# Moving token sums, a turned tile and the last store in a float32 attention and gated-MLP kernel on one Trainium2 core

## The chip, the cores and the metric

The kernel runs on one core of a Trainium2 chip. A core has TensorE (PE, matrix products into the banks of PSUM), VectorE (DVE), ScalarE (ACT), GpSimd (POOL) and SyncE (SP); SP, ACT and POOL also issue the DMA transfers. The engines run at the same time, each works through its own instructions in order, and semaphores make one wait for another. The metric is the device time of one execution in microseconds (us). Before the change it is 1393.94 us, the median of three runs.

## The reference

Two layers, each an attention block A and a gated MLP block B, on 2048 tokens of 512 features, all in float32. `layernorm` takes mean and variance over the last axis.

```python
def A(x, wqkv, wo):                       # 32 heads of 16
    q, k, v = split(x @ wqkv)
    pq, pk = phi(q), phi(k)               # phi(t) = (t + 1 if t > 0 else exp(t)) + 1e-6
    kv = einsum("bhsd,bhse->bhde", pk, v)
    z = einsum("bhsd->bhd", pk)
    num = einsum("bhqd,bhde->bhqe", pq, kv)
    den = einsum("bhqd,bhd->bhq", pq, z)[..., None] + 1e-6
    return merge(num / den) @ wo

def B(x, w_in, w_sp, b_sp, w_out):        # w_in 512 x 1792, w_sp 2048 x 2048
    z = gelu(x @ w_in)
    z1, z2 = z[..., :896], layernorm(z[..., 896:])
    g = w_sp @ z2 + b_sp[:, None]
    return (z1 * g) @ w_out

x = x + A(layernorm(x)); x = x + B(layernorm(x))
x = x + A(layernorm(x)); x = x + B(layernorm(x))
```

## The kernel before

**Numbers.** A float32 operand is split into a high part (ACT, `high`, L101) and the rest (DVE or POOL, `low`, L104); `mm3` (L115 to L117) makes one product out of three matmuls on these parts. So each operand costs PE a wait for ACT first, and for DVE at the third matmul.

**Memory.** `Slots` hands out tiles by hand: 22 pages (`pg`, 128 x 512 floats), 6 quads (`qd`), 4 bigs (`bg`) and 8 PSUM banks. A freed tile goes to the end of its list; who gets it next waits for its last users. The order of every engine's work is the order of the calls in the Python code.

**Stages.** The 2048 tokens are 16 blocks of 128. Each layer has these stages:

- `P1`: blocks are loaded, normalised and turned (`T`, in a high and a low half), then multiplied by the weights for K and Q. `start` (first layer) loads the first blocks and eight weight pieces, fills the wait of PE with `idle` matmuls on constants (L434), and interleaves the splits of the pieces (`wk.piece`) with the first blocks. Blocks 0 to 2 of the first layer are turned on PE (L247), all others by a store, a load and a transpose on DVE (L286).
- `P2`: steps `s` = 1 to 18. A step takes block `s` through `b`, block `s - 1` through `c` (a product, an addition L643, statistics, `c3` with a store and the turning) and block `s - 2` through `d` (turned and split into `xT`, one quad each for the high and low parts of four blocks). Block `s - 3` goes through `e` (24 matmuls with 448 columns, two gelus L700, statistics L222), block `s - 4` through `e4` (normalised). Products `f` with the other half of `w_in` are made for four blocks at a time.
- `P4`: 56 steps of products with `w_sp`, then `o(i)` for 16 blocks: product, addition L1198, store L1200. `join` starts the next layer's `P1` in the last steps of the first layer: `T(0)` in step 14 and `T(1)` in step 15.

**The seven products.** In the second layer (`self.seven`) the `f` products of the last eight blocks are made as seven products of half-size parts (P1 to P7). Four of these need sums of tokens of two blocks: block 8 + k, kept in `xT[2]`, and block 12 + k, just turned (`y`). In `d_low` of blocks 12 to 15, steps 14 to 17, `block_sums` (L755 to L758) writes the four sums; the full value of block 8 + k comes from `whole`, which adds its high and low part on POOL (L743) a step ahead. `block_parts(m, p)` splits the sums into the quads `Tp[m]`, in two halves `p`. `side(s)` sets what of this a step does: products P1 and P2 (`P1(g)`, `P2(g)`, six matmuls each, L791 to L793), with copies (L799), the addition L813 and gelus (L733); the splits; and `fetch_sum`, three DMAs on POOL's queue (L773), which bring weight sums stored in DRAM by the first layer. `tail` then makes P3 to P7, and each product waits for its `Tp` and its fetched sums.

**Sums of `w_sp`.** In the first layer `sums.tick()` (steps 8 to 18 and some of `P4`) loads pieces of `w_sp`, adds them on POOL (L978) and stores the sums.

Of the kernel before, what the change touches and what calls it, by code (L numbers as in the profile page):

```python
# [10 lines left out]
F32 = mybir.dt.float32  # L11
# [42 lines left out]
def mixer_kernel(ctx: ExitStack, tc: tile.TileContext, x_in, wqkv, wo_d, win1_d, win2_d, wsp_d, bsp_d, wout_d,  # L54
# [236 lines left out]
    class P1:  # L291
# [124 lines left out]
        def start(self):  # L416
# [19 lines left out]
            idle(10)  # L436
# [3 lines left out]
            self.wk.piece()  # L440
            self.T_high(0)
            idle(4)
# [3 lines left out]
            self.wk.piece()  # L446
# [122 lines left out]
    class P2:  # L569
        def __init__(self, p1):  # L570
# [8 lines left out]
            self.S, self.T, self.Tp = {}, {}, {}  # L579
# [92 lines left out]
        def d_low(self, i):  # L672
# [3 lines left out]
            if self.seven and n == 3:  # L676
                self.block_sums(k, b)
            home.put(b)
# [34 lines left out]
        def f(self):  # L713
# [8 lines left out]
            if f == NF - 1 and not (self.seven and n == 3):  # L722
                quads.put(*self.xT.pop(n))
# [15 lines left out]
        def whole(self, k):  # L739

            h, l = (t[:, :, k * P:(k + 1) * P].bitcast(F32) for t in self.xT[2])
            self.xr = pages.get([P, 4, P])
            nc.gpsimd.tensor_tensor(self.xr, h, l, op=OP.add)  # L743

        def block_sums(self, k, y):


            p, o = divmod(k, 2)
# [4 lines left out]
            x = self.xr  # L753
# [5 lines left out]
            pages.put(x)  # L759
# [42 lines left out]
        def P1(self, g):  # L802
            if g == 0:
                self.X, self.C = [], []
            self.X.append(banks.get(PAGE))
            self.product(self.X[g], "P1", g, start=True)
            self.C.append(self.copied(self.X[g]))

        def P2(self, g):
            y = banks.get(PAGE)  # L810
            self.product(y, "P2", g, start=True, stop=True)
            t = self.C[g]
# [48 lines left out]
        def side(self, s):  # L861

            if s == 14:
                self.P1(0)
                self.P1(1)
            elif s == 15:
                self.P1(2)
                self.P2(0)
                self.fetch_sum(4)
            elif s == 16:  # L870
                self.P2(1)
                self.P2(2)
# [12 lines left out]
            if 13 <= s < 17:  # L885
                self.whole(s - 13)

        def run(self, sums):
            w1 = self.win1
            for s in range(1, NT + 3):  # L890
# [16 lines left out]
                else:  # L907
# [37 lines left out]
                w1.fetch()  # L945
                if s > 7:
# [54 lines left out]
    class P4:  # L1001
# [189 lines left out]
        def o(self, i):  # L1191
# [6 lines left out]
            nc.vector.tensor_add(x, x, b)  # L1198
# [119 lines left out]
```

## Time and profile before

| | before |
|---|---|
| device time, three runs | 1392.9, 1393.94, 1395.38 us; median 1393.94 us |
| the profiled execution | 1392.76 us, its span 1391.0 us |
| PE (matmuls) busy | 1383.0 us, 99% of the span, 6252 matmuls |
| DVE busy | 908.8 us, 65% |
| ACT busy | 595.1 us, 43% |
| POOL busy | 429.2 us, 31% |
| chain of work that ended last | PE 96%, DVE 2%, ACT 1%, POOL 1%, issue 1% |
| DMA | 233.57 MB, mean 168 GB/s |

The span is the time from the first to the last instruction of the profile; the device time of the same execution is 1.76 us longer. In the rows below, a row of the timeline gives the start and the duration in us, the engine (PEld is the load of a matmul's weights, `SPq` an issue of a DMA by SP), the line of the kernel, what is written and read, a count, and in brackets for how long the engine was idle before and what ended that. Neighbouring instructions of one kind can be merged into one row with their count. PE's busy time is modelled: matmuls overlap, so two starts may lie closer together than one matmul lasts.

### The profile page before, as it was taken

The page shows a single profiled execution, that of the slowest core. Times are in us where ns is not written, and L with a number is a line of the kernel's source. Part 1 is how long each engine was busy: PE and PEld are TensorE (multiplying, and loading weights), DVE is VectorE, ACT ScalarE, POOL GpSimd, SP SyncE. Part 2 cuts the span into 40 slices and gives each one's busy share as a digit, 9 for nine tenths or more (in the row PEclk, how much of TensorE's full clock was granted, in tenths as well). Part 3 has the DMA queues.
Part 4 walks back from the last instruction along what each step waited for, and adds up shares of the span by engine and source line. Part 5 has one row for each costly group of instructions (what it writes and reads, how often), then busy time and mean ns, then how long its engine had stood idle before and what let it go on. Part 6 is the DMA issues. An engine that isn't in the chain of part 4 may idle for free.

```text
span 1391.0 us, 17707 instructions
## 1 busy us (share of the span) xinstructions
PE 1383.0 (99%) x6252; PEld 1159.9 (83%) x6252; DVE 908.8 (65%) x1305; ACT 595.1 (43%) x922; POOL 429.2 (31%) x518
## 2 busy tenths in 40 slices
PE   9999999999999999999999999999999999999998
PEld 7888888888888888888888888888878888888887
DVE  6785777853755587666667767876666345776642
ACT  6674543444442234241366755444454432342410
POOL 3343344544135541431023424432320001123310
PEclk9999999999999999999999999999999999999999
DMA  5541256766678864357745313555454323434442
GB/s 174 171 132 59 91 167 224 260 228 211 212 246 287 297 228 137 122 203 241 266 130 177 112 45 122 174 175 173 124 187 152 106 91 129 174 129 159 167 145 90
DMA packets 148313, 233.57 MB, mean 168 GB/s; under 512 B 12416, under 2 KB 54144, under 8 KB 148224
## 3 DMA queue, kind: packets, MB, share of 16 engines
q1 hardware_dynamic: 144768, 226.15, 49.0%
q0 software_dynamic: 1728, 3.15, 0.8%
q10 hardware_dynamic: 1728, 3.15, 0.6%
q8 instruction: 49, 0.80, 0.2%
q14 instruction: 40, 0.33, 0.1%
HBM read 161.35 MB, written 71.04 MB: 167 GB/s over the span
## 4 chain that ended last, share of the span: by engine, by line
PE 96%; DVE 2%; ACT 1%; POOL 1%; issue 1%; ACTq 0%; POOLq 0%
PE bank L117 18%; PE bank L116 18%; PE bank L115 18%; PE bank L1105 13%; PE bank L1104 13%; PE bank L1103 13%; PE bank L247 1%; PE bank L793 0%; PE bank L792 0%; PE bank L791 0%; DVE st L222 0%; PE bank L434 0%; ACT qd L101 0%; ACT pg L235 0%; DVE pg L286 0%
## 5 line engine op out<-in xcount | busy, mean ns | idle before, releaser
L1104 PE MATMUL bank<-qd,pg 128*128 128x512 f32 x800 | 311.2, 389 | 0.0
L1105 PE MATMUL bank<-qd,pg 128*128 128x512 f32 x800 | 311.2, 389 | 0.0
L1103 PE MATMUL bank<-qd,pg 128*128 128x512 f32 x800 | 311.2, 389 | 0.0
L1069 DVE TENSOR_TENSOR qd<-qd,qd 128x1024 fp32r<-128x1024 f32 x112 | 158.4, 1414 | 138.7 <-ACT qd L1062 138.5
L1062 ACT ACTIVATE qd<-qd 128x1024 fp32r<-128x1024 f32 x112 | 118.6, 1059 | 235.9 <-DMA qd<-s 96.5
L1125 POOL TENSOR_TENSOR bg<-bg,pg 128x512 f32<-128x512 f32 x56 | 78.2, 1399 | 327.6 <-DMA pg<-z 302.9
L1104 PEld LDWEIGHTS bank<-qd,pg 128*128 128x128 f32 x800 | 150.2, 188 | 31.4
L1103 PEld LDWEIGHTS bank<-qd,pg 128*128 128x128 f32 x800 | 150.2, 188 | 31.3
L1105 PEld LDWEIGHTS bank<-qd,pg 128*128 128x128 f32 x800 | 150.2, 188 | 30.8
L117 PE MATMUL bank<-qd,pg 128*128 128x512 f32 x384 | 149.9, 390 | 0.0
L226 POOL TENSOR_SCALAR rs<-mv 128x1 f32<-128x1 f32 x96 | 38.5, 401 | 333.5 <-DVE mv L224 320.3
L978 POOL TENSOR_TENSOR pg<-pg,pg 128x512 f32<-128x512 f32 x64 | 93.7, 1464 | 93.8 <-DMA pg<-in_wsp_dram 85.4
L235 ACT ACTIVATE pg<-pg,nb,rs 128x512 f32<-128x512 f32 x63 | 51.1, 811 | 161.8 <-POOL nb L229 155.6
L115 PE MATMUL bank<-qd,pg 128*128 128x512 f32 x288 | 112.3, 390 | 0.0
L116 PE MATMUL bank<-qd,pg 128*128 128x512 f32 x288 | 112.2, 390 | 0.0
L115 PE MATMUL bank<-bg,qd 128*128 128x448 f32 x256 | 94.2, 368 | 1.6 <-ACT qd L101 1.6
L117 PE MATMUL bank<-bg,qd 128*128 128x448 f32 x256 | 93.6, 366 | 0.1
L116 PE MATMUL bank<-bg,qd 128*128 128x448 f32 x256 | 93.6, 366 | 0.0
L101 ACT ACTIVATE pg<-pg 128x512 fp32r<-128x512 f32 (+1 forms) x83 | 51.0, 616 | 96.5 <-DVE pg L286 51.9
L115 PE MATMUL bank<-wo,qd 128*128 128x512 f32 x224 | 87.1, 389 | 0.0
L116 PE MATMUL bank<-wo,qd 128*128 128x512 f32 x224 | 87.1, 389 | 0.0
L117 PE MATMUL bank<-wo,qd 128*128 128x512 f32 x224 | 87.1, 389 | 0.0
(156 smaller groups left out, 2689.7 us busy)
## 6 DMA issues: line engine op xcount, KB each, us to landing
qd<-s SPq DMA_DIRECT2D x64, 512.0 KB, 3.4
qd<-in_wsp_dram SPq DMA_DIRECT2D x48, 512.0 KB, 4.2
pg<-in_wsp_dram SPq DMA_DIRECT2D x64, 256.0 KB, 5.0
s<-pg SPq DMA_DIRECT2D x64, 256.0 KB, 4.8
pg<-x SPq DMA_DIRECT2D x64, 256.0 KB, 3.3
pg<-z SPq DMA_DIRECT2D x56, 256.0 KB, 3.7
x<-pg SPq DMA_DIRECT2D x48, 256.0 KB, 2.6
z<-pg SPq DMA_DIRECT2D x44, 256.0 KB, 2.9
```

Source lines behind the costliest of these rows:

```text
L101: nc.scalar.activation(h, src, AF.Copy)
L115: nc.tensor.matmul(out, ah, bh, start=start, stop=False)
L116: nc.tensor.matmul(out, ah, bl, start=False, stop=False)
L117: nc.tensor.matmul(out, al, bh, start=False, stop=stop)
L235: nc.scalar.activation(y, x, AF.Identity, bias=nb, scale=rs)
L978: nc.gpsimd.tensor_tensor(t, a, b, op=OP.add)
L1062: nc.scalar.activation(w[:, 0], r, AF.Copy)
L1069: nc.vector.tensor_sub(w[:, 1], r, w[:, 0].bitcast(F32))
L1103: m(out, h[:, o], w[:, 0, j, :], start=start, stop=False, skip_group_check=True)
L1104: m(out, h[:, o], w[:, 1, j, :], start=False, stop=False, skip_group_check=True)
L1105: m(out, l[:, o], w[:, 0, j, :], start=False, stop=stop, skip_group_check=True)
L1125: nc.gpsimd.tensor_tensor(u, u, z1, op=OP.mult)
```

## The change

- `start`: 8 and 2 idle matmuls where there were 10 and 4; the second weight piece is split before the high half of block 0's turned tile, where it came after its low half.
- Second layer, steps 13 to 18: `whole` goes away. `d_low` of blocks 12 to 15 only keeps `y` (`held`); `block_sums` takes it a step later, steps 15 to 18, after `d` and before `e4`, and adds the high and low part of block 8 + k itself, on DVE.
- `side`: P1(g) in steps 14, 15, 16 and P2(g) in steps 15, 16, 17, one each (before: two P1 in step 14, one of each in step 15, two P2 in step 16). All splits are in steps 17 (two) and 18 (six), where they were in steps 16, 17 and 18. The three fetches go to steps 16, 17, 18 (before 15, 16, 17). `xT[2]` is given back in step 18.
- First layer: one `sums.fetch()` already in step 7.
- `join`: `T(1)` of the next layer comes before `o(15)` instead of after it.
- The last output block of the second layer is added and stored in two halves of 256 columns, one store on SP's queue and one on ACT's.

```diff
-            idle(10)
+            idle(8)
             self.ln_a(0)
             self.ln_a(1)
             self.ln_b(0)
             self.wk.piece()
+            self.wk.piece()
             self.T_high(0)
-            idle(4)
+            idle(2)
             banks.put(b)
             pages.put(m, f)
             self.T_low(0)
-            self.wk.piece()
             self.ln_b(1)
...
             if self.seven and n == 3:
-                self.block_sums(k, b)
-            home.put(b)
+                self.held.append((k, b))
+            else:
+                home.put(b)
...
-        def whole(self, k):
-
+        def block_sums(self):
+
+
+            if not self.held:
+                return
+            k, y = self.held.popleft()
+            x = pages.get([P, 4, P])
             h, l = (t[:, :, k * P:(k + 1) * P].bitcast(F32) for t in self.xT[2])
-            self.xr = pages.get([P, 4, P])
-            nc.gpsimd.tensor_tensor(self.xr, h, l, op=OP.add)
-
-        def block_sums(self, k, y):
-
-
+            nc.vector.tensor_add(x, h, l)
...
-            if s == 14:
-                self.P1(0)
-                self.P1(1)
-            elif s == 15:
-                self.P1(2)
-                self.P2(0)
+            if 15 <= s < 18:
+                self.P2(s - 15)
+            if 14 <= s < 17:
+                self.P1(s - 14)
+            if s == 16:
                 self.fetch_sum(4)
-            elif s == 16:
-                self.P2(1)
-                self.P2(2)
-                self.fetch_sum(2)
-                for m in (2, 3):
-                    self.block_parts(m, 0)
             elif s == 17:
                 self.last_f(2)
-                self.block_parts(2, 1)
-                self.block_parts(3, 1)
+                self.block_parts(2, 0)
+                self.block_parts(3, 0)
+                self.fetch_sum(2)
+            elif s == 18:
+                quads.put(*self.xT.pop(2))
+                for m, p in ((2, 1), (3, 1), (4, 0), (4, 1), (1, 0), (1, 1)):
+                    self.block_parts(m, p)
                 self.fetch_sum(3)
-            elif s == 18:
-                for m in (4, 1):
-                    for p in range(2):
-                        self.block_parts(m, p)
-            if 13 <= s < 17:
-                self.whole(s - 13)
...
+                if s >= 15:
+                    self.block_sums()
                 if s >= 4:
                     self.e4(s - 4)
...
+                if s == 7:
+                    sums.fetch()
                 if s > 7:
                     sums.tick()
...
-            nc.vector.tensor_add(x, x, b)
+            out = xs[2 * self.L + 2, i]
+            if self.L == 1 and i == NT - 1:
+                for issue, s in ((nc.sync, slice(0, 256)), (nc.scalar, slice(256, 512))):
+                    nc.vector.tensor_add(x[:, s], x[:, s], b[:, s])
+                    issue.dma_start(out[:, s], x[:, s])
+            else:
+                nc.vector.tensor_add(x, x, b)
+                nc.sync.dma_start(out, x)
             banks.put(b)
-            nc.sync.dma_start(xs[2 * self.L + 2, i], x)
...
+                if i == NT - 1 and nxt is not None:
+                    nxt.T(1)
                 self.o(i)
...
-            if i == 15:
-                nxt.T(1)
```

More of the change, by code (lines that the diff above doesn't have):

```diff
@@ L578, in __init__ @@
             self.seven = self.L == 1
-            self.S, self.T, self.Tp = {}, {}, {}
+            self.held = deque()
+            self.S, self.T, self.Tp, self.X = {}, {}, {}, {}
         def loadx(self, i):
@@ L721, in f @@
                 mm3(b, (w.h[:, f, c, :], w.l[:, f, c, :]), (h[:, c, :], l[:, c, :]), c == 0, c == 3)
-            if f == NF - 1 and not (self.seven and n == 3):
+            if f == NF - 1 and not (self.seven and n >= 2):
                 quads.put(*self.xT.pop(n))
@@ L758, in block_sums @@
             V.tensor_sub(t[4], x[:, 2:4, :], t[2])
-            pages.put(x)
+            pages.put(x, y)
         def block_parts(self, m, p):
@@ L811, in P2 @@
             self.product(y, "P2", g, start=True, stop=True)
-            t = self.C[g]
+            t = self.C
             nc.vector.tensor_add(t, t, y)
```

7 lines of the change are left out of this document (2 added, 5 removed).

## The prediction

> **What bounds the kernel now.** I read the page first, then the list of waits of TensorE (PE), then the order of time around each place where PE waits, then the start and the end of the program.
>
> ```profile
> span 1391.0 us, 17707 instructions
> ...
> PE 1383.0 (99%) x6252; PEld 1159.9 (83%) x6252; DVE 908.8 (65%) x1305; ACT 595.1 (43%) x922; POOL 429.2 (31%) x518
> ```
>
> ```profile
> PE bank L434 <- DVE pg L429: 2.3, 1, 2.3
> PE bank L115 <- ACT qd L101: 1.6, 1, 1.6
> ```
>
> The first fence is the page's table of engines, the second the list of PE's waits (total, times, longest). PE is busy for 1383.0 of 1391.0 us, and the change removes only four of its matmuls, idle ones. So it can win only where PE waits: about 8 us, of which 2.3 are the lead-in, 1.6 one wait for ACT, and most of the rest lies behind the last matmul. Busy time hides short waits, though: a matmul lasts 0.39 us, while the next can start after 0.23 us. I therefore look at starts, not at busy time. Starts that lie too far apart occur in only four places: the start, the join of the two layers (near 702 us), step 17 to 18 of the second layer's middle stage (near 1008 us), and the end.
>
> ```profile
> 1000.74 0.36 PE L115 MATMUL bank<-bg,qd 128*128 128x448 f32 x1
> ...
> 1005.60 0.39 PE L115 MATMUL bank<-qd,bg 128*128 128x512 f32 x1
> ...
> 1008.13 0.39 PE L117 MATMUL bank<-qd,bg 128*128 128x512 f32 x1
> 1010.16 0.47 PE L115 MATMUL bank<-bg,qd 128*128 128x448 f32 x1 [1.64 <-ACT qd L101]
> ...
> 1015.53 0.40 PE L115 MATMUL bank<-qd,bg 128*128 128x512 f32 x1
> ```
>
> These rows of PE's timeline (start, duration, line) begin the groups `e(14)` (24 matmuls, 1000.74 to 1005.60, so 4.86 us) and the last plain group of block 2 (12 matmuls; 1005.60 to the twelfth at 1008.13 are eleven spacings of 0.23), then `e(15)` and the group after it. `e(15)` could follow 0.23 us after 1008.13, at 1008.36, and be over 4.86 us later, at 1013.22. It is over at 1015.53. So 2.31 us are lost here, the largest sum that can be won anywhere.
>
> **Why `e(15)` waits.** It needs block 15 turned and split (`d(15)`).
>
> ```profile
> 1001.27 0.32 SPq L97 DMA_DIRECT2D pg<-yt  x1
> 1002.83 1.23 DVE L813 TENSOR_TENSOR pg<-pg,bank 128x512 f32<-128x512 f32 x2
> 1006.23 2.22 DVE L104 TENSOR_TENSOR qd<-pg,qd 128x512 fp32r<-128x512 f32 x2 [2.17 <-ACT qd L101]
> 1008.38 1.06 DVE L286 STREAM_TRANSPOSE pg<-pg 128x512 f32<-128x512 f32 x1
> 1009.48 0.63 ACT L101 ACTIVATE qd<-pg 128x512 fp32r<-128x512 f32 x1 [2.75 <-DVE pg L286]
> DMA to landing us min/median/max: 2.3/2.4/2.9
> ```
>
> The load of block 15 was issued at 1001.27 and had landed by 1001.27 + 2.9 = 1004.2. Its transpose starts only at 1008.38, because VectorE (DVE) has two splits of token sums ahead of it (L104 x2, 1006.23 to 1008.45), which themselves waited 2.17 us for their ScalarE (ACT) halves; in the code those halves are queued behind the gelus of both product sums (L813 x2). So 4.2 us pass between landing and transpose, in queues and not in data.
>
> **The change at this place, -2.31 us.** It moves both early splits behind `d(15)`, and one product pair (6 matmuls) from before `c(15)` to after `e(14)`. PE then reaches `c(15)` 6 x 0.23 = 1.4 us sooner. The new work on DVE per step is one addition of high and low halves; POOL's addition L743 goes.
>
> ```profile
> 978.05 0.42 DVE L755 TENSOR_TENSOR pg<-pg,pg 128x256 f32<-128x256 f32 x1
> 979.52 1.14 DVE L222 BATCH_NORM_STATS2 st<-z_z 128x6 f32<-128x448 f32 x2
> 993.33 0.69 DVE L643 TENSOR_TENSOR pg<-pg,bank 128x512 f32<-128x512 f32 x1 [0.87 <-PE bank L117]
> 999.45 0.69 DVE L104 TENSOR_TENSOR qd<-pg,qd 128x512 fp32r<-128x512 f32 x1 [3.48 <-ACT qd L101]
> ```
>
> I walk the new order. L643 of `c(15)` waits for PE, so it moves from 993.33 to 991.9; the same 6.1 us after it, at 998.0, comes L104 of `d(14)`. Behind it DVE now has, in order: that L104 (0.69), the new addition (priced as an L104 of the same size, 0.69), four token sums (978.05 to 979.52, 1.47), two statistics and their end (1.3), one product sum L813 (0.63). That is 4.8 us, so the transpose of block 15 starts at 1002.8; 1.06 for it, 0.64 for ACT, 0.69 for DVE: split done near 1005.3. ACT has one gelu, one store and one copy in between, about 1.6 us, beside the transpose; allowing another 0.6 gives 1005.9. PE asks at 1008.36. The cover is 2.5 us; if it were gone, each microsecond beyond would come back as wait. `e(14)` needs `d(14)` at about 999.4 (six matmuls sooner) and has it at 998.7.
>
> What is late next: six splits in step 18, not two. They go behind the statistics of block 15.
>
> ```profile
> 1018.50 2.45 DVE L104 TENSOR_TENSOR qd<-pg,qd 128x512 fp32r<-128x512 f32 x4
> 1018.68 0.55 POOL L226 TENSOR_SCALAR rs<-mv 128x1 f32<-128x1 f32 x1 [1.47 <-DVE mv L224]
> 1021.02 1.70 POOL L773 DMA_DIRECT2D pg<-win_sums  x3
> DMA to landing us min/median/max: 3.2/4.1/5.0
> ```
>
> Before, the splits start 1018.50 - 1015.53 = 3.0 us after the end of `e(15)`; so now at 1013.22 + 3.0 = 1016.2, at 0.61 each: the first done at 1016.8, the sixth at 1019.9. PE meanwhile has 12 + 18 matmuls, 6.9 us, and asks for the first (P6) at 1020.1. Cover 3.3 us.
>
> The three fetches of stored sums on POOL for P7 move behind the last normalisation factors: POOL's chain from L226 to the next fetch takes 1021.02 - 1018.68 = 2.3 us, so 1016.3 + 2.3 = 1018.6 for the first issue, 4.1 to land, 1022.7. P7 asks at 1020.1 + 4.1 = 1024.2, and for the second 1.4 us later. Cover 1.5 us, or 0.6 at the longest landing of 5.0. I cost it at nothing, and keep it as a rival. The fetches for P3 and P6 each go a step later too: issued near 1002 and 1009, landed 1.7 + 5.0 later at the latest, by 1009 and 1016, where PE asks at 1016.0 and 1020.1.
>
> **The join, -0.25 us.**
>
> ```profile
> 698.99 0.69 DVE L1198 TENSOR_TENSOR pg<-pg,bank 128x512 f32<-128x512 f32 x1 [1.68 <-PE bank L117]
> 701.37 0.69 DVE L104 TENSOR_TENSOR pg<-pg,pg 128x512 fp32r<-128x512 f32 x1 [0.70 <-ACT pg L101]
> 701.74 0.40 PE L116 MATMUL bank<-qd,pg 128*128 128x512 f32 x1
> 702.45 0.39 PE L115 MATMUL bank<-qd,pg 128*128 128x512 f32 x1
> ```
>
> From 701.74 to 702.45 pass 0.71 us where 0.46 would do: L117 waits for the split of the second turned tile, done at 702.06. Moved ahead of the last output group, that tile no longer stands behind L1198, which waits for PE until 698.99. The split is then over near 699.7; L1198 slips at most as far, and its bank comes up again only after the seven others. The first fetch of the first layer's sums puts three loads on SP's queue a step sooner, ahead of that step's load of a block and of a turned tile, which come three issues later once; POOL then adds without waiting for data. PE has no uneven start in that whole stage, so I find nothing to win there and take the slack it implies as cover: nothing.
>
> **The end, -0.1 us.**
>
> ```profile
> 1387.09 0.69 DVE L1198 TENSOR_TENSOR pg<-pg,bank 128x512 f32<-128x512 f32 x1 [4.07 <-PE bank L117]
> out_dram<-pg SPq DMA_DIRECT2D x2, 256.0 KB, 2.0
> ```
>
> One addition of 0.69 becomes two of 256 columns, 0.42 each and some 0.35 apart (as L755): the second ends near 1387.87, 0.1 later than before, but carries half the bytes. Two bounds: a half lands as slowly as a whole, +0.1; the half takes 0.35 us less (a transfer of some 0.7 us is the most that fits the 2.0), -0.25. I take the middle.
>
> **The start, +0.1 us, the least certain term.**
>
> ```profile
> 2.32 4.45 PE L434 MATMUL bank<-pg,ones 128*128 128x512 f32 x10 [2.32 <-DVE pg L429]
> 7.24 0.60 ACT L101 ACTIVATE pg<-bank 128x512 fp32r<-128x512 f32 x1 [0.94 <-PE bank L247]
> 7.73 0.62 ACT L101 ACTIVATE qd<-pg 128x512 fp32r<-128x512 f32 x1
> 15.91 0.81 ACT L235 ACTIVATE pg<-pg,nb,rs 128x512 f32<-128x512 f32 x1 [2.83 <-POOL nb L229]
> 17.08 0.60 PE L247 MATMUL bank<-ident,pg 128*128 128x128 f32 x4
> L97 SPq DMA_DIRECT2D pg<-in_wqkv_dram x2: 431/432/432, 2.1 to 2.6; - x2
> DMA to landing us min/median/max: 3.5/4.3/5.1
> ```
>
> Ten idle matmuls take 4.45 us, the last running on past its turn: one every 0.43. Two fewer before the first transposes let these come 0.4 us sooner, once the normalised tile is there. But ACT now splits the second weight piece ahead of the turned tile (7.24), and that piece must have landed. The last row is of the first two pieces: 3.5 and 5.1 us. If the second again lands at 2.6 + 5.1 = 7.7, the turned tile starts one spacing (7.24 to 7.73, 0.49) after it, at 8.22, 1.0 late; PE gets 0.1 back where it no longer waits for that piece's low half, +0.87. If it lands as fast as the first (6.1), PE gains 0.5 at first, but the transposes at 17.08 need L235, done at 16.72 and bound by a later load: at most -0.24. With the middle, 4.3: the piece is there at 6.9, the turned tile starts at 7.4 instead of 7.24, and the removed wait leaves +0.1.
>
> **The sum** against the profiled execution (span 1391.0, its own time 1392.76): -2.31 - 0.25 - 0.1 + 0.1 = -2.56, so 1390.2. The median of the three runs, 1393.94, is 1.18 above that execution: 1391.4. The bounds give -3.05 (1390.9) and -1.6 (1392.3).
>
> **Rivals.**
> 1. The start gains in full: -2.31 - 0.25 - 0.1 - 0.24 = -2.9, 1391.0. For it: the piece's landing is one transfer in one execution. Against: 5.1 us is what was measured.
> 2. The wait moves to P7: a fetch that lands at 5.0 and a POOL chain 1.5 us longer leave PE waiting 0.9 us, 1392.3. For it: only 0.6 us of cover in that corner. Against: POOL lost its four additions.
> 3. PE stays slow at the start. The idle matmuls come every 0.43 us, all later ones every 0.23 us: some 4.1 us of unbroken work, from 2.3 to 6.4, went before full speed. Now PE runs out of idle matmuls at 2.32 + 8 x 0.43 = 5.8, and pauses again from about 7.0 until the turned tile is split (8.2). If the count begins anew there, matmuls stay at 0.43 until 12.3 at least: ten of them, +2.0 us, 1393.4. If a pause breaks it once more, to about 16.4, there are 19, +3.8 us: 1395.2, slower than before. It decides at 2.56 / 0.20 = 13 slow matmuls after 6.4.
> 4. The change doesn't do what it says: `d(15)` is still late because the product sums hold DVE. That needs 2.5 us more than counted; with half the stall left, 1392.6.
>
> [...]
>
> **Chances.** Forecast 0.60, rival 1 0.18, rivals 2 and 4 0.07, rival 3 0.09, something unseen that costs more 0.06. This kernel's runs lie 1392.9 to 1395.38, so 0.2% (2.8 us, a time of 1391.15) is about what a measurement can tell from no change, and the forecast lies almost on it: half of its 0.60 falls on either side. Faster: 0.30 + 0.16 + 0.01 = 0.47. Slower: the unseen 0.06 and half of rival 3, 0.05: 0.11. Within: 0.42. Range: the bounds 1390.9 to 1392.3, with 1.3 us for the runs' own spread on either side, to 1389.6 and 1393.6; that takes in rivals 1, 2 and 4 and part of 3.
>
> **What would show it.** In the profile after: no wait of PE before `e(15)`, whose first matmul follows the one before by 0.23 us, and the transpose of block 15 well before it; no gap near 702; no new wait at P6 or P7; matmuls every 0.23 us from about 6.4 on; the second piece's landing against the start of the turned tile. Wrong would be: a wait of PE between 1008 and 1036 above 0.5 us, or a first transposition of the third tile (17.08) that comes later than 17.95.

## The result and the profile after

| | before | after |
|---|---|---|
| device time, median | 1393.48 us (12 runs, 1392.75 to 1395.38) | 1390.43 us (12 runs, 1390.0 to 1391.24) |
| ratio of the times | | 0.9977, 95% interval 0.9969 to 0.9986 |
| the profiled execution, its span | 1392.76, 1391.0 us | 1390.0, 1388.2 us |

The change makes the kernel faster by 0.23%, 3.05 us of median. The first fence is the page of the changed kernel: its span and the busy time of the engines. The second is its list of PE's waits (total, times, longest).

```profile
span 1388.2 us, 17699 instructions
...
PE 1381.7 (100%) x6248; PEld 1159.4 (84%) x6248; DVE 909.8 (66%) x1310; ACT 595.2 (43%) x922; POOL 425.4 (31%) x514
```

```profile
PE bank L434 <- DVE pg L429: 2.3, 1, 2.3
PE bank L115 <- ACT pg L101: 0.4, 1, 0.4
```

The span has lost 2.8 us and PE's busy time 1.3 (1383.0 to 1381.7), so by this page only 1.5 us of the gain was idle time of PE. Busy time can't tell more: it also holds the four idle matmuls that went, and delays shorter than a matmul's modelled length (0.39 us). The wait of 1.6 us for `qd` is gone; a new one of 0.4 us stands at the start. The next fence is PE's timeline of the changed kernel where `e(15)` begins (start, duration, engine, line).

```profile
1007.75 0.39 PE L117 MATMUL bank<-qd,bg 128*128 128x512 f32 x1
1007.98 0.36 PE L115 MATMUL bank<-bg,qd 128*128 128x448 f32 x1
```

The first matmul with 448 columns, L115 at 1007.98, follows 0.23 us behind the last plain one: no wait at all. The same view over POOL, SP, DVE and ACT shows why (POOL's first row is the normalisation factor of block 15, SP's row the load of block 15):

```profile
991.59 0.69 DVE L644 TENSOR_TENSOR pg<-pg,bank 128x512 f32<-128x512 f32 x1 [0.35 <-PE bank L117]
...
993.46 0.22 POOL L226 TENSOR_SCALAR rs<-mv 128x1 f32<-128x1 f32 x1 [1.36 <-DVE mv L224]
...
994.73 0.81 ACT L235 ACTIVATE pg<-pg,nb,rs 128x512 f32<-128x512 f32 x1 [1.75 <-POOL nb L229]
...
996.10 0.69 DVE L104 TENSOR_TENSOR qd<-pg,qd 128x512 fp32r<-128x512 f32 x1 [1.82 <-ACT qd L101]
...
997.92 0.32 SPq L97 DMA_DIRECT2D pg<-yt  x1
...
1000.85 1.10 DVE L286 STREAM_TRANSPOSE pg<-pg 128x512 f32<-128x512 f32 x1
...
1003.15 0.69 DVE L104 TENSOR_TENSOR qd<-pg,qd 128x512 fp32r<-128x512 f32 x1 [1.20 <-ACT qd L101]
```

Block 15 is split at 1003.15 + 0.69 = 1003.84, 4.1 us before PE asks. POOL makes the factor (L226) right behind the statistics, where before it came at 996.80; ACT's L235, the load of block 15 and the split of `d(14)` (996.10) all come some 3.3 us sooner, though PE reached `c(15)` (L644 at 991.59, L643 at 993.33 before) only 1.7 us sooner. That is more than the prediction gave them, and the experiments ask where it is from.

Three more places of the changed kernel. At the join (first fence) L117 follows L116 by 0.23 us; the turned tile is split at 699.70, ahead of L1199 in DVE's queue. In step 18 (second fence) the six splits run from 1015.01 to 1018.66, and the fetches start at 1018.05 (three issues for P7, then three for P5); PE enters P6 (1019.67) and P7 (1023.75) without an uneven start. At the end (third fence, and the rows of the list of DMA issues: count, KB, median us to landing) the last addition is in two.

```profile
699.01 0.69 DVE L104 TENSOR_TENSOR pg<-pg,pg 128x512 fp32r<-128x512 f32 x1 [0.70 <-ACT pg L101]
...
699.62 0.68 DVE L1199 TENSOR_TENSOR pg<-pg,bank 128x512 f32<-128x512 f32 x1
...
701.75 0.39 PE L116 MATMUL bank<-qd,pg 128*128 128x512 f32 x1
701.98 0.39 PE L117 MATMUL bank<-qd,pg 128*128 128x512 f32 x1
```

```profile
1015.01 3.65 DVE L104 TENSOR_TENSOR qd<-pg,qd 128x512 fp32r<-128x512 f32 x6
...
1018.05 3.28 POOL L774 DMA_DIRECT2D pg<-win_sums  x6
...
1019.67 0.39 PE L792 MATMUL bank<-qd,pg 128*128 128x512 f32 x1
...
1023.75 0.39 PE L792 MATMUL bank<-qd,pg 128*128 128x512 f32 x1
```

```profile
1384.56 0.75 DVE L1196 TENSOR_TENSOR pg<-pg,bank 128x256 f32<-128x256 f32 x2 [4.07 <-PE bank L117]
...
out_dram<-pg SPq DMA_DIRECT2D x1, 128.0 KB, 1.8
out_dram<-pg ACTq DMA_DIRECT2D x1, 128.0 KB, 1.8
```

The start of the changed kernel:

```profile
2.32 3.78 PE L434 MATMUL bank<-pg,ones 128*128 128x512 f32 x8 [2.32 <-DVE pg L429]
...
5.99 1.38 ACT L101 ACTIVATE qd<-pg 128x512 fp32r<-128x512 f32 x2 [3.98 <-DMA pg<-in_wqkv_dram]
...
7.28 0.58 ACT L101 ACTIVATE pg<-bank 128x512 fp32r<-128x512 f32 x1
...
7.91 0.50 PE L115 MATMUL bank<-qd,pg 128*128 128x512 f32 x1 [0.36 <-ACT pg L101]
...
17.06 0.60 PE L247 MATMUL bank<-ident,pg 128*128 128x128 f32 x4
```

ACT splits both weight pieces (x2) and the turned tile begins at 7.28, almost as before (7.24); the first product at 7.91 (7.95), the transposes at 17.06 (17.08). Nothing is won or lost here in these two executions.

**Where the time went.** I pair each matmul of the changed kernel with the one of before that stands equally far from the last, and read how much later it starts. The table gives the growth of this shift over four stretches, for each run below as well (all against before's profiled execution, us); "clock" is the time at which the trace's record of PE's granted clock goes to full speed, "wait" is PE's wait before `e(15)` beyond the usual spacing, "end" the time from the last matmul to the end of the span.

| run | time | clock | to 67 us | 67 to 672 | join | 887 to 1053 | wait | end |
|---|---|---|---|---|---|---|---|---|
| before | 1392.76 | 6.42 | 0 | 0 | 0 | 0 | 1.80 | 3.95 |
| after | 1390.0 | 6.79 | +0.01 | +0.01 | -0.29 | -2.25 | 0 | 3.68 |
| e1_seven | 1391.17 | 8.45 | +0.63 | +0.22 | -0.01 | -2.46 | 0 | 3.93 |
| e2_join | 1394.48 | 8.22 | +0.62 | -0.01 | -0.29 | +1.40 | 1.80 | 3.94 |
| e3_start | 1392.98 | 6.60 | +0.38 | +0.03 | -0.01 | -0.20 | 1.84 | 3.94 |
| e4_tail | 1392.54 | 6.32 | -0.04 | +0.17 | -0.01 | -0.09 | 1.80 | 3.68 |
| e5_late_splits | 1390.17 | 5.35 | -0.44 | +0.15 | -0.01 | -2.36 | 0 | 3.95 |
| e6_early_splits | 1390.06 | 7.48 | +0.11 | +0.01 | -0.29 | -2.25 | 0 | 3.68 |
| e7_spread | 1393.4 | 7.60 | +0.62 | +0.45 | -0.01 | -0.43 | 1.30 | 3.95 |
| e8_few_idle | 1392.42 | 13.99 | +2.41 | +0.05 | -0.29 | -2.24 | 0 | 3.68 |
| e9_turn_first | 1390.76 | 6.72 | +0.79 | +0.04 | -0.29 | -2.27 | 0 | 3.68 |
| e10_dve_add | 1391.99 | 6.22 | -0.08 | +0.77 | -0.01 | -1.46 | 0.58 | 3.95 |
| e11_late_fetch | 1391.43 | 6.86 | +0.22 | +0.17 | -0.02 | -1.70 | 0.26 | 3.94 |
| e12_old_order | 1389.97 | 7.00 | -0.03 | +0.01 | -0.29 | -2.27 | 0 | 3.69 |

For the change: +0.02 - 0.29 - 2.25 - 0.27 = -2.79, the difference of the two spans. The -2.25 is more than the wait of 1.80: in before the first three matmuls of `e(15)` also took 1.03 us (1010.16 to 1011.19), in part since L117 waited for DVE's half of the split, where the changed kernel's take 0.61 (1007.98 to 1008.59). The runs that leave the middle stage alone (e3, e4) differ from before there by -0.20 and -0.09, so a few tenths in that column are the run's own.

### The profile page after: what moved, and what is told of

Same layout as the page of the kernel before. It is cut to its first block, busy times and chain, and to the rows that moved or that the text cites. A ratio compares the mean times of both kernels' runs of the same rounds, so it can differ in the third digit from the quotient of the medians.

```text
span 1388.2 us, 17699 instructions
## 1 busy us (share of the span) xinstructions
PE 1381.7 (100%) x6248; PEld 1159.4 (84%) x6248; DVE 909.8 (66%) x1310; ACT 595.2 (43%) x922; POOL 425.4 (31%) x514
## 4 chain that ended last, share of the span: by engine, by line
PE 99%; DMA 0%; SPq 0%; DVE 0%; ACT 0%; issue 0%; DVEq 0%
PE bank L117 19%; PE bank L116 19%; PE bank L115 19%; PE bank L1100 13%; PE bank L1099 13%; PE bank L1098 13%; PE bank L794 1%; PE bank L793 1%; PE bank L792 1%; PE bank L247 1%; DMA pg<-in_wqkv_dram 0%; SPq L97 0%; DVE pg L104 0%; ACT qd L101 0%; DVE qd L104 0%; PE bank L516 0%
## 5 line engine op out<-in xcount | busy, mean ns | idle before, releaser
L117 PE MATMUL bank<-qd,pg 128*128 128x512 f32 x384 | 149.7, 390 | 0.1
L226 POOL TENSOR_SCALAR rs<-mv 128x1 f32<-128x1 f32 x96 | 38.2, 398 | 340.5 <-DVE mv L224 337.1
L235 ACT ACTIVATE pg<-pg,nb,rs 128x512 f32<-128x512 f32 x63 | 51.0, 810 | 154.6 <-POOL nb L229 148.4
L115 PE MATMUL bank<-qd,pg 128*128 128x512 f32 x288 | 112.4, 390 | 0.4 <-ACT pg L101 0.4
L116 PE MATMUL bank<-qd,pg 128*128 128x512 f32 x288 | 112.1, 389 | 0.0
L115 PE MATMUL bank<-bg,qd 128*128 128x448 f32 x256 | 94.0, 367 | 0.0
L116 PE MATMUL bank<-bg,qd 128*128 128x448 f32 x256 | 93.6, 366 | 0.0
L117 PE MATMUL bank<-bg,qd 128*128 128x448 f32 x256 | 93.4, 365 | 0.0
L115 PE MATMUL bank<-wo,qd 128*128 128x512 f32 x224 | 87.1, 389 | 0.0
L116 PE MATMUL bank<-wo,qd 128*128 128x512 f32 x224 | 87.1, 389 | 0.0
L117 PE MATMUL bank<-wo,qd 128*128 128x512 f32 x224 | 87.1, 389 | 0.0
```

The source lines that it names most:

```text
L115: nc.tensor.matmul(out, ah, bh, start=start, stop=False)
L116: nc.tensor.matmul(out, ah, bl, start=False, stop=False)
L117: nc.tensor.matmul(out, al, bh, start=False, stop=stop)
L235: nc.scalar.activation(y, x, AF.Identity, bias=nb, scale=rs)
```

## The experiments

Two questions: which part of the change brought which term, and what made block 15 late. My first theory was the prediction's: DVE's two early splits, waiting for ACT halves that are queued behind two gelus, hold up the transpose. Each diff is against before, unless it says otherwise, and is an excerpt: three dots stand for lines left out. Runs for which one time is given are single executions; there I go by the stretches of the table and not by the total.

**The seven products alone** (the whole of the change in steps 13 to 18, with start, join, first layer and last store as before).

```diff
-            if s == 14:
-                self.P1(0)
-                self.P1(1)
...
+            if 15 <= s < 18:
+                self.P2(s - 15)
+            if 14 <= s < 17:
+                self.P1(s - 14)
...
+                if s >= 15:
+                    self.block_sums()
...
```

> The kernel before with the second layer's steps 13 to 18 of the changed kernel alone (token sums a step later, splits in steps 17 and 18, products P1 and P2 one each per step). My theory, each gap is its own: the wait before e(15) near 1008 us is gone, the gap near 702 us (0.25 us) and the end are as before; last matmul 2.2 to 2.3 us sooner than the 1387.05 us of before, time 2.2 us less (0.16%). Rival, the parts lean on one another: the wait comes back in part, and the time is less than 1.5 us below before.

Measured: 1390.65 us (11 runs, 1389.9 to 1391.27) beside 1393.12 of before, ratio 0.998, interval 0.9971 to 0.9989. The wait before `e(15)` is gone, the uneven start at the join is there. So this part carries most of the gain; the rest of the change is too small for its ratio to tell it from this. Its profiled execution is only 1.6 us shorter than before's, because the start (+0.63) and the first layer (+0.22) took longer in it.

**The join alone.**

```diff
+                if i == NT - 1 and nxt is not None:
+                    nxt.T(1)
                 self.o(i)
...
-            if i == 15:
-                nxt.T(1)
```

> The kernel before with T(1) of the second layer ahead of the last output group of the first, and nothing else. My theory: L117 no longer waits near 702 us, all later matmuls start 0.25 to 0.3 us sooner up to the wait near 1008 us, and that wait keeps its length, because its chain begins with PE too; span 1390.7. Rival: the wait near 1008 us is set by DMA and takes the 0.3 us back; span 1391.0.

Measured: 1394.48 us. The join gives its -0.29, but the whole is slower than before, by the start (+0.62) and by something new behind the wait; neither expectation has that. The windows views of this run and of before (stretch, length; busy time and count of PE, PEld, DVE, ACT, POOL; granted clock, DMA share, GB/s) show 3.6 us that begin 1.2 us behind that wait in this run, which comes first, and 0.8 us behind it in before:

```profile
1011.60:1015.20 3.60, 3.60 (x11) 3.19 (x11) 3.35 (x8) 2.14 (x5) 1.19 (x2) 0.53 0.19 73
```

```profile
1011.00:1014.60 3.60, 3.60 (x18) 3.29 (x19) 3.53 (x9) 2.52 (x6) 0.82 (x2) 1.00 0.19 73
```

In this run PE's granted clock is 0.53 of full speed on average there, and 11 matmuls fit where before had 18. The wait is as long as in before (1.80 us), but at that clock the run lost another 1.40 us in this stage (by the table). The edit does not touch this stage; in this one run the wait was followed by a loss beyond its own length.

**Only the order of the splits** (two in step 17, six in step 18; the products, sums and fetches as before).

```diff
-                for m in (2, 3):
-                    self.block_parts(m, 0)
             elif s == 17:
                 self.last_f(2)
-                self.block_parts(2, 1)
-                self.block_parts(3, 1)
+                self.block_parts(2, 0)
+                self.block_parts(3, 0)
                 self.fetch_sum(3)
             elif s == 18:
-                for m in (4, 1):
-                    for p in range(2):
-                        self.block_parts(m, p)
+                for m, p in ((2, 1), (3, 1), (4, 0), (4, 1), (1, 0), (1, 1)):
+                    self.block_parts(m, p)
```

> The kernel before with only the order of the eight splits changed: two in step 17 (of blocks 12 and 13), six in step 18; token sums, products and POOL's additions as before. My theory, the wait before e(15) stood in the queues of DVE and ACT behind the two early splits: the transpose of block 15 starts near 1004.2 us, after the two product sums, its split is done by 1007, and the whole 2.3 us are won. Rival, PE's earlier arrival at c(15) and POOL's freed time were needed: block 15 is split only near 1009, and at most 1.2 us are won.

Measured: 1390.17 us; the wait is gone (-2.36 in the middle), and the transpose of block 15 starts at 1004.10, as my theory expected (1004.2). PE's timeline of this run:

```profile
1007.87 0.39 PE L117 MATMUL bank<-qd,bg 128*128 128x512 f32 x1
1008.10 0.36 PE L115 MATMUL bank<-bg,qd 128*128 128x448 f32 x1
```

`e(15)` follows by 0.23 us. Moving four splits by one step is enough for the whole term.

**The other way round**: the changed kernel with two splits put back into step 16, ahead of `d(15)`.

```diff
             if s == 16:
                 self.fetch_sum(4)
+                self.block_parts(2, 0)
+                self.block_parts(3, 0)
             elif s == 17:
                 self.last_f(2)
-                self.block_parts(2, 0)
-                self.block_parts(3, 0)
```

> The changed kernel with the first two splits put back into step 16, ahead of block 15's turn. If late splits are what cured the wait, it comes back: the transpose of block 15 (1000.85 us in the changed kernel) goes to about 1004.4, its split is done near 1006.8, still ahead of 1008.0, so no more than 0.3 us should return by my count. Rival, the splits alone made the wait: 1.5 us or more return, span 1389.7 or above.

Measured: 1390.06 us, no wait, -2.25 in the middle as in the changed kernel; the transpose of block 15 starts at 1004.46 (expected 1004.4). The rival fails. So late splits are enough, and not needed: something else in the new order is enough as well. The first theory tells half of the story.

**One product pair per step, alone.** The other thing that the prediction named is the pair of products moved behind `c(15)`.

```diff
-            if s == 14:
-                self.P1(0)
-                self.P1(1)
-            elif s == 15:
-                self.P1(2)
-                self.P2(0)
+            if 15 <= s < 18:
+                self.P2(s - 15)
+            if 14 <= s < 17:
+                self.P1(s - 14)
+            if s == 15:
                 self.fetch_sum(4)
             elif s == 16:
-                self.P2(1)
-                self.P2(2)
                 self.fetch_sum(2)
...
```

(The bookkeeping of banks and copies goes with it, and `xT[2]` is given back in step 18.)

> Before, with P1 and P2 spread one per step over steps 14 to 17 alone: the two early splits stay in step 16, the sums stay in d_low with POOL's addition. Theory A (the early splits are late because their ScalarE halves stand behind the gelus of two product sums in one step; one of these gone and PE 1.4 us earlier at c(15), the transpose of block 15 comes before PE asks): no wait of 0.5 us or more before e(15), about 2.3 us less than before at 1050 us. Theory B (the sums in d_low and the addition on POOL are part of the delay): a wait of 0.5 to 2 us remains before e(15).

Measured: 1393.4 us, a wait of 1.30 us: theory B. The spread takes 0.5 us off the wait and no more. POOL's and PE's rows of this run:

```profile
994.15 1.85 POOL L773 DMA_DIRECT2D pg<-win_sums  x3
...
996.02 1.30 POOL L743 TENSOR_TENSOR pg<-qd,qd 128x512 f32<-128x512 f32 x1
...
997.41 0.23 POOL L226 TENSOR_SCALAR rs<-mv 128x1 f32<-128x1 f32 x1
...
1010.76 0.47 PE L115 MATMUL bank<-bg,qd 128*128 128x448 f32 x1 [1.14 <-ACT qd L101]
```

This names the missing half. The factor L226 of block 15 waits on POOL behind three issues of a fetch and the addition L743, however early `c(15)` is. The timeline of before, POOL with one row each of DVE and ACT, has the same queue:

```profile
993.53 1.85 POOL L773 DMA_DIRECT2D pg<-win_sums  x3 [0.23 <-issue]
...
994.78 0.18 DVE L224 BATCH_NORM_AGGREGATE mv<-st 128x2 f32<-128x6 f32 x1
...
995.40 1.31 POOL L743 TENSOR_TENSOR pg<-qd,qd 128x512 f32<-128x512 f32 x1
...
996.80 0.23 POOL L226 TENSOR_SCALAR rs<-mv 128x1 f32<-128x1 f32 x1
...
998.08 0.82 ACT L235 ACTIVATE pg<-pg,nb,rs 128x512 f32<-128x512 f32 x1 [4.95 <-POOL nb L229]
```

The statistics are ready at 994.78 + 0.18 = 994.96 and L226 starts at 996.80, 1.84 us late; ACT stands idle 4.95 us for the factor, with the copy of `d(14)` and the store and load of block 15 behind it. New theory (C): the delay begins on POOL. The next two runs take away one part of that queue each.

**POOL's addition moved to DVE, alone.**

```diff
-            nc.gpsimd.tensor_tensor(self.xr, h, l, op=OP.add)
+            nc.vector.tensor_add(self.xr, h, l)
```

> Before, with the addition of high and low part (whole, L743) on DVE instead of POOL, and nothing else. Theory C (the delay begins on POOL: three fetch issues, 993.53 to 995.38, and L743, 995.40 to 996.71, stand ahead of the normalisation factor L226 of block 15, whose statistics are ready at 994.96; ACT's L235 waits for it, and behind L235 stand the copy of d(14) and the load of block 15): L226 starts near 995.4 instead of 996.8, the load of block 15 is issued near 999.9 instead of 1001.27, and the wait of 1.84 us before e(15) shrinks to 0.4 to 1.2 us, since DVE has 0.7 us more to do. Theory A (only the order of DVE's splits and PE's products counts): the wait stays at 1.7 us or more.

Measured: 1391.99 us, and a wait of 0.58 us, inside theory C's 0.4 to 1.2. Its rows on POOL, SP and PE:

```profile
996.41 0.23 POOL L226 TENSOR_SCALAR rs<-mv 128x1 f32<-128x1 f32 x1
...
1000.89 0.32 SPq L97 DMA_DIRECT2D pg<-yt  x1
...
1009.52 0.47 PE L115 MATMUL bank<-bg,qd 128*128 128x448 f32 x1 [0.42 <-ACT qd L101]
```

This run stood 0.59 us later than before when it came to this stage, for a reason told below, so L226 at 996.41 is about 1.0 us sooner than in before, and the load of block 15 likewise (1000.89 against 1001.27).

**The three fetches one step later, alone.**

```diff
                 self.P2(0)
-                self.fetch_sum(4)
...
                 self.P2(2)
-                self.fetch_sum(2)
+                self.fetch_sum(4)
...
                 self.block_parts(3, 1)
-                self.fetch_sum(3)
+                self.fetch_sum(2)
...
                         self.block_parts(m, p)
+                self.fetch_sum(3)
```

> Before, with each of the three fetches of stored sums one step later (16, 17, 18 instead of 15, 16, 17), and nothing else; the early splits, the pairs of P1 and P2, and the addition on POOL stay. Theory C (the delay begins on POOL): L743 and the factor L226 come 1.4 to 1.8 us sooner, the load of block 15 is issued by 999.9, and the wait of 1.84 us before e(15) shrinks to 0 to 0.5 us: a gain of 1.3 to 1.9 us at 1050 us from one moved line. Theory A (only the order of DVE's splits and PE's products counts): the wait stays at 1.7 us or more.

Measured: 1391.43 us, a wait of 0.26 us, inside theory C's 0 to 0.5.

```profile
995.37 0.22 POOL L226 TENSOR_SCALAR rs<-mv 128x1 f32<-128x1 f32 x1 [0.54 <-DVE mv L224]
...
999.83 0.32 SPq L97 DMA_DIRECT2D pg<-yt  x1
...
1008.86 0.47 PE L115 MATMUL bank<-bg,qd 128*128 128x448 f32 x1
```

L226 now waits for DVE's statistics and not for POOL. Three DMA issues of 1.85 us moved one step remove 1.54 of the 1.80 us of wait, with the early splits and the pairs of products untouched. Theory C stands. The last 0.26 us of wait go with other parts of the change, and which of them takes it away is not separated.

**The start alone.**

```diff
-            idle(10)
+            idle(8)
...
             self.wk.piece()
+            self.wk.piece()
             self.T_high(0)
-            idle(4)
+            idle(2)
...
             self.T_low(0)
-            self.wk.piece()
             self.ln_b(1)
```

> Before, with the new start alone (8 and 2 idle matmuls, the second weight piece split ahead of the turned tile). Theory A (the order is worth nothing, the start moves only with the time at which the clock goes to full speed and with the landing of the second piece): the first proper matmuls stand within 0.3 us of before's (7.95), and the whole stays at 1392.5 to 1393.9 us, with the waits at 702 and before e(15) as before. Theory B (rival 3 of the prediction, the shorter idle work breaks the count to full speed): matmuls still 0.43 us apart after 10 us, 2 us or more lost, 1395 us or more.

Measured: 1392.98 us; the first product at 8.29, 0.34 late, a little over theory A's bound, and far from theory B's 2 us.

```profile
7.12 0.63 ACT L101 ACTIVATE qd<-pg 128x512 fp32r<-128x512 f32 x1 [0.25 <-DMA pg<-in_wqkv_dram]
7.66 0.58 ACT L101 ACTIVATE pg<-bank 128x512 fp32r<-128x512 f32 x1
```

ACT waited for the second piece, which landed at 7.1, and split the turned tile 0.54 us behind it. In the changed kernel's profile the piece was there before ACT had done the first one. So the same start costs 0.0 in one execution and 0.38 in another, by one landing.

**The last store alone.**

```diff
+            out = xs[2 * self.L + 2, i]
+            if self.L == 1 and i == NT - 1:
+                for issue, s in ((nc.sync, slice(0, 256)), (nc.scalar, slice(256, 512))):
+                    nc.vector.tensor_add(x[:, s], x[:, s], b[:, s])
+                    issue.dma_start(out[:, s], x[:, s])
...
```

> Before, with the last store split over two queues alone. From the last matmul's end to the end of the span before has 3.95 us. Theory A (two stores issued side by side each carry half the bytes and end sooner): 3.6 to 3.8 us. Theory B (a half lands as slowly as a whole, the second addition comes 0.1 us later): 4.0 to 4.1 us. The rest as before, 1392.5 to 1393.9 us.

Measured: 1392.54 us; 3.68 us from the last matmul to the end, -0.27, the same as in the changed kernel. Each half lands 1.8 us after its issue, where the whole took 2.0.

**Fewer idle matmuls still**, in the changed kernel.

```diff
-            idle(8)
+            idle(4)
...
-            idle(2)
+            idle(0)
```

> The changed kernel with 4 and 0 idle matmuls instead of 8 and 2: PE now rests from about 4.1 to 6.0 us and from 6.7 to 7.9 us. Theory A (the step to full speed comes at a time of its own, here 5.4 to 8.5 us in the runs so far, whatever the pause): matmuls 0.23 us apart from at most 9 us on, start within 0.7 us of before's, 1390.0 to 1391.5 us. Theory B (a pause begins the count anew): matmuls 0.43 us apart until 10 us or later, start 1 to 2.5 us later, 1391.5 to 1393 us.

Measured: 1392.42 us; theory A falls. PE's timeline of this run:

```profile
13.64 0.56 PE L117 MATMUL bank<-qd,pg 128*128 128x512 f32 x1
14.04 0.39 PE L115 MATMUL bank<-qd,pg 128*128 128x512 f32 x1
14.26 0.40 PE L116 MATMUL bank<-qd,pg 128*128 128x512 f32 x1
```

From 13.64 to 14.04 pass 0.40 us, then 0.22: matmuls stay at half pace until here (the clock's step is at 13.99), and the start is 2.4 us late. This is the loss of the prediction's rival 3, near its price of 2.0 us, called up by taking four and two more idle matmuls away (theory B). The change itself, with its step at 6.79, stays clear of it.

**A start meant to be better**: the changed kernel with the turned tile's high half ahead of the second piece.

```diff
             self.wk.piece()
-            self.wk.piece()
             self.T_high(0)
+            self.wk.piece()
             idle(2)
```

> The changed kernel with the high half of block 0's turned tile split ahead of the second weight piece again, the fewer idle matmuls kept. Theory A (in the changed kernel the turned tile waits on ACT for the second piece, whose landing moves by half a microsecond from run to run): the first proper matmul comes near 7.4 instead of 7.9 us, the whole start is 0.2 to 0.5 us sooner wherever the clock goes to full speed before 8.5 us, and the median is 1389.9 to 1390.3 us. Theory B (the normalised third block or the slow clock sets the pace of the start): no gain at 67 us, 1390.4 us or more.

Measured: 1390.88 us (11 runs, 1390.51 to 1391.14), ratio 0.9984, interval 0.9975 to 0.9993; the start +0.79. Theory A fails: I had looked at ACT only. DVE's and PE's rows:

```profile
8.21 0.69 DVE L104 TENSOR_TENSOR qd<-pg,qd 128x512 fp32r<-128x512 f32 x1 [0.69 <-ACT qd L101]
```

```profile
9.56 0.50 PE L117 MATMUL bank<-qd,pg 128*128 128x512 f32 x1 [1.11 <-DVE pg L104]
```

The first product does come sooner (7.71), but on DVE the second piece's low half (8.21) now stands before the turned tile's, and L117 waits 1.11 us for that one.

**The old order with the fewer idle matmuls**: the changed kernel with the second piece behind `T_low(0)` again.

```diff
             self.wk.piece()
-            self.wk.piece()
             self.T_high(0)
...
             self.T_low(0)
+            self.wk.piece()
             self.ln_b(1)
```

> The changed kernel with the splits of the start in the order of before (first piece, turned tile high, turned tile low, second piece) and the 8 and 2 idle matmuls of the change. Theory A (the fewer idle matmuls are what helps at the start, and the second piece ahead of the turned tile is not needed and costs as often as it lands late): first proper matmul near 7.7 us, L117 no later than 8.5, the matmuls near 67 us 0.1 to 0.3 us sooner than in the changed kernel for the same step of the clock, median 1390.0 to 1390.4 us. Theory B (the second piece's low half, now behind the turned tile's, makes PE wait as in before): first matmul near 7.7 but no gain at 67 us, 1390.4 us or more.

Measured: 1390.0 us (11 runs, 1389.55 to 1390.11) beside 1392.99 of before, ratio 0.9978, interval 0.9968 to 0.9987. It is the lowest median here, and the one with the least spread, but its ratio is that of the changed kernel, so the two can't be told apart. Its profile has the first product at 7.85 and L117 at 8.58, both a little later than I expected, and the start at -0.03 with the clock's step at 7.00. What the runs do say is that the second piece ahead of the turned tile is not needed.

## Why the prediction was right, point by point

The forecast was 1391.4, the measured median is 1390.43, inside the range. The direction, the place and the order of the terms were right.

- **The middle stage**, forecast -2.31, measured -2.25. The size was right, and the route half right. The failed step is "the same 6.1 us after it, at 998.0, comes L104 of `d(14)`": measured are 991.59 and 996.10, 4.5 us. Those 6.1 us held POOL's queue of three issues and one addition, which the prediction listed as moved and removed and costed at nothing. Without that queue the transpose started at 1000.85, not at 1002.8, and the cover was 4.1 us, not 2.5. That the error lay on the safe side was luck. The two remedies are each sufficient (the splits moved alone; everything else with the splits early), so neither alone can be called the cause: before, a late factor and two late splits stood one behind the other, and the sum was 1.80 us more than PE's work covered.
- **What is late next**: nothing, as forecast. The six splits began at 1015.01, forecast 1016.2. The first fetch for P7 was issued at 1018.05, forecast 1018.6, and landed 3.2 us later, 2.5 us before P7 at 1023.75; forecast cover 1.5. Rival 2 did not come, nor rival 4.
- **The join**, forecast -0.25, measured -0.29 in the change and in all four runs made from it, and in the run with the join alone.
- **The end**, forecast -0.1 between +0.1 and -0.25, measured -0.27: near the lower bound, but made up otherwise. By the trace's issues and landings the last store is issued 0.82 us after the last matmul's end (before 0.75), so the second addition costs 0.07, about the 0.1 of the forecast; it lands after 1.78 us instead of 2.05, 0.26 less, where the bounds had 0 and 0.35 (in before's windows view the DMA share is 0.77 in the stretch from 1388.60 to 1389.50 us, so 0.7 us of the 2.05); and the program ends 1.08 us after that landing, in before 1.15, which the forecast did not have and which stays open.
- **The start**, forecast +0.1, measured +0.01. The mechanism was right in kind: the turned tile follows the second piece by half a microsecond (0.54 in the start-alone run). Only the landing differed, 7.1 there and before ACT was free in the changed kernel; which of the two the profiled execution would have was luck. Rival 1 asked for a gain of 0.24 here and had none; rival 3's price was shown, but by another edit, and its count of some 4.1 us of unbroken work does not hold (see the last section).
- **The first layer's fetch**, costed at nothing. Against before's profile that came out (+0.01), but that execution was a good one in this place. Of the nine profiles without the early fetch, the stretch from 67 to 672 us grows by -0.01 to +0.77, 0.22 in the mean; of the five with it, by 0.01 to 0.05. The reason for the larger part stands in POOL's rows of before, of the run with the addition on DVE (where it cost most) and of the changed kernel:

```profile
226.91 2.65 POOL L978 TENSOR_TENSOR pg<-pg,pg 128x512 f32<-128x512 f32 x2 [4.33 <-DMA pg<-in_wsp_dram]
```

```profile
227.90 2.66 POOL L978 TENSOR_TENSOR pg<-pg,pg 128x512 f32<-128x512 f32 x2 [5.42 <-DMA pg<-in_wsp_dram]
...
230.65 0.22 POOL L226 TENSOR_SCALAR rs<-mv 128x1 f32<-128x1 f32 x1
```

```profile
222.58 2.65 POOL L973 TENSOR_TENSOR pg<-pg,pg 128x512 f32<-128x512 f32 x2
```

  POOL's additions wait for a load of `w_sp`, and the next normalisation factor (L226) stands behind them, as it stood behind the fetches in the second layer. The load came 1 us later in the second of these runs, and there PE's shift grows from -0.07 at 224 us to +0.69 at 278; the `e` group between them, at 233, has the only uneven starts in that stretch. With the fetch a step sooner POOL waits for nothing. Over all nine profiles without the early fetch the growth between 228 and 250 us follows POOL's wait: none after waits of 3.79, 3.84, 4.33, 4.37 and 4.58 us, then 0.17 after 4.91, 0.09 after 4.92, 0.42 after 5.24 and 0.76 after 5.42, so 0.16 in the mean; the five with it have none. One of those without growth (4.58, the start alone) has the new start, so the start is not what helps here. The rest of the column is something else: in the seven products alone, the late splits and the late fetch 0.13 to 0.16 us are lost between 197 and 205 us, ahead of the load of `w_sp` (issued at 221.58 in before), and why stays open. The early fetch alone was not run.
- **From the sum to the median.** The sum forecast 1390.2 for the profiled execution, and it took 1390.0. The rest of the miss is the 1.18 us that I added for the distance of before's median from its profiled execution. After the change that distance is 0.43, and before's own median fell from 1393.94 in three runs to 1393.48 in twelve.
- **The chances.** Faster by over 0.2% had 0.47, against 0.42 for no change to tell; the ratio came out at 0.23%, on the line that the forecast named.

## What to carry to other kernels

When an engine waits for data that has long landed, follow the queue of every engine that the data passes, POOL and its DMA issues too: here the issues of three fetches, 1.85 us on an engine that was busy 31% of the time, were over at 995.38 and made up 1.54 of the 1.80 us of a wait of PE that began at 1008.36. Where two delays stand one behind the other, removing either may remove most or all of the wait, so test each alone before naming the cause. A row that costs nothing in one profile may be a wait that happened not to last in that execution: look at how long the transfer under it takes in several (here POOL waited 3.79 to 5.42 us for one load in nine profiles).

## What the hardware showed beside this

- **The clock's step at the start came at different times.** The trace's record of the granted clock goes to full speed between 5.35 and 8.45 us in thirteen profiles (13.99 in the one with too few idle matmuls). In before it does at 6.42 us; its idle matmuls ahead of that come every 0.43 us, and its matmuls later every 0.23 us. With the old start the first stretch follows it: -0.44 us at 5.35, -0.08 at 6.22, 0 at 6.42, +0.22 at 6.86, and 0.62 to 0.63 from 7.60 on. With the changed kernel's start 6.79 and 7.48 gave +0.01 and +0.11, and 7.00 gave -0.03 with the old order of the splits and the fewer idle matmuls. So the fewer idle matmuls seem to make the start less dependent on the step; this rests on three profiles, and a fourth (the start alone, 6.60) has +0.38 for the late landing told above. The step does not follow a fixed length of unbroken work, as rival 3 had it: in both the late splits and the seven products alone PE works from 2.32 on without a pause, and the step came 3.0 us after that in the one and 6.1 us in the other. What sets its time is not shown.
- **A wait of 1.80 us was followed by half clock, once.** In the run with the join alone the record has half clock for 3.413 us, beginning at 1011.74 (0.53 on average from 1011.60 to 1015.20), 1.35 us after the wait ended (1010.39). In before the clock stayed at 1.00 behind a wait of the same 1.80 us (windows view, 1007.50 to 1018.20). Nor is there a loss of that size behind the waits of 1.84 us (the start alone), 1.80 (the last store alone) and 1.30 (the pairs spread): their stretch of the table has -0.20, -0.09 and -0.43. So the length of the wait alone does not decide it, and what does is not shown. It may be why before's runs reach 1395.38 and the changed kernel's end at 1391.24: of before's 56 timed executions on record nine lie at 1394.73 or above and none between 1393.94 and that. But those runs have no profile, so this is argued and not shown.
